# The first chunk's scores and feed-forward products from unsplit float32 operands, and a transpose in PE's transpose mode, in a bucketed attention and feed-forward kernel

## Chip, core and metric

One core of a Trainium2 chip runs the whole kernel. The metric is device time in microseconds (us) of one execution. The engines are named as in the profile: PE does matrix products (PEld are its weight loads), DVE, ACT and POOL are the vector, scalar and general engines, SP issues DMAs.

## What is computed

Attention over 4 batches, 8 heads, 768 positions and a head width of 64, in which a query sees only keys of its own hash bucket, and behind it a feed-forward block of 3072 tokens, width 512, inner width 2048:

```python
q_bits = (np.einsum('bhsd,dk->bhsk', q, proj) > 0)      # 6 bits a position, k likewise
mask = q_bucket[:, :, :, None] == k_bucket[:, :, None, :]
scores = np.where(mask, scale * np.matmul(q, k.transpose(0, 1, 3, 2)), -1000000000.0)
attn = np.exp(scores - max) / (sum + 1e-09)
x = np.matmul(attn, v)          # as [3072 tokens, 8 heads x 64]
h = x @ w_in
out = (0.5 * h * (1.0 + erf(h / sqrt(2)))) @ w_out
```

Inputs are float32, the two weights arrive as float64. The result is close to float32, so most products are made from 16-bit halves.

## The kernel before

**Passes and units.** The work goes in passes (`passes`): the first 256 queries of batch 0, the other 512 of batch 0, and then batches 1 to 3 whole. A pass goes through the eight heads, and a head through units of 128 queries by 768 keys (`unit`): 16 units in the first pass, 32 in the second, 48 in each other one, 192 in all. Queries are grouped in chunks of 256; the feed-forward part works on one chunk after the other, twelve of them.

**A head** (`head`) loads q and k of the head, transposed, as one tile of 128 partitions (`raw`, in the first pass `rawe`), takes the largest absolute value (L545), sums it over partitions on PE (L502), makes a power-of-two scale in four small DVE steps (L505 to L520), a 16-bit high half (L550) and low halves (L569 to L585), and copies halves to the other partitions by DVE, ACT, POOL or DMA (L552). The halves are projected on the hash vectors (L610), ACT takes signs (L616), and four small steps write them as extra rows beside q and k, so that a score product also adds the mask. The operands are the four tiles Aq, Ak, Bq and Bk. The first pass uses eight sets of them, of which six stay for the second pass; the two other heads are prepared again there. The sets beyond lie in the memory of x, or in a pool that is released (`go_late`) before the tiles `h` and `g` of the feed-forward part are made.

**A unit** makes scores by four 16-bit products (L824, L825), the row maximum (L828), two small steps (L832, L837), exponentials with their sum on ACT (L840), and the reciprocal of the sum (L850). Then there are two ways. The "whole" way (`whole_turn`, for all four pairs of heads in the first pass and three in the second) stays in float32: it scales the identity by the reciprocals (tile `dr`), multiplies the exponentials by it on PE, six products of 128 by 128 (L897), which transposes and divides at once, and ACT or DVE copies the result to `pt`. The other way makes high and low halves on two engines (L853, L856) and transposes them by DMA. `values` multiplies by v: twelve float32 products (L945) or 36 16-bit ones (L954) for a pair of heads and a chunk, given out in three steps, and writes x as two halves (L974, L981).

**Weights** (`weight_pair`) are decoded from float64 to float32 on DVE in place (L667 to L677), squared sums on PE give a scale (L690), and each of eight blocks of each weight is scaled into a buffer `o`, rounded and subtracted into two 16-bit halves that overwrite the float32 values.

**Feed-forward.** A chunk goes in two groups of eight inner blocks. A hidden step is twelve 16-bit products 256 wide (L1128), ACT evacuates two steps at a time (L1138) and applies Gelu to the group in the one buffer `h` (L1162), the result is split into halves `g` (L1172, L1176), and an output step is six products 512 wide (L1200). Output sums keep two of the four PSUM banks `hp` from the first group to the drain (L1221); scores of projections, transposes, values and hidden steps share the others. Before the first output product all of w_out must be split, and before a hidden product its block of w_in.

**Order.** No engine's order is written by hand. `Plan` lists steps with an engine or several that may do it, a cost, a key and the steps they need, runs through them in a model of the engines, and writes the instructions in the order found; free steps of lowest key go first. Keys are the unit's number with an offset from the table `PAR`; feed-forward steps on PE have keys from 1000 (`LATE`) on, so they come only where no attention product is ready. Each engine runs its instructions in the written order.

## Time and profile before

| | us |
|---|---|
| median of three runs | 924.03 |
| lowest and highest | 920.8, 924.16 |
| the profiled execution | 922.43 |
| its span, first to last instruction | 920.3 |

| engine | busy us | share of the span |
|---|---|---|
| PE | 852.7 | 93% |
| PEld | 577.0 | 63% |
| DVE | 732.2 | 80% |
| ACT | 615.6 | 67% |
| POOL | 376.1 | 41% |

The mean clock granted to PE is 0.983 of full speed. In the profile a line of slices gives the busy share of 40 equal parts of the span in tenths. A row of a stage has the stage's ends, its length, then busy time and number of instructions of PE, PEld, DVE, ACT and POOL, the granted clock, the share of DMA and GB/s. A row of the timeline has start, duration, engine, line, operation, output and input tile, form and count, and in brackets idle time before it and what ended it. A row of groups has line, engine, operation, tiles, form and count, then busy time and mean ns, then idle time before it. Durations on PE overlap; a float32 product shows as two records.

### The profile page before, as it was taken

The page shows a single profiled execution, that of the slowest core. Times are in us where ns is not written, and L with a number is a line of the kernel's source. Part 1 is how long each engine was busy: PE and PEld are TensorE (multiplying, and loading weights), DVE is VectorE, ACT ScalarE, POOL GpSimd, SP SyncE. Part 2 cuts the span into 40 slices and gives each one's busy share as a digit, 9 for nine tenths or more (in the row PEclk, how much of TensorE's full clock was granted, in tenths as well). Part 3 has the DMA queues.
Part 4 walks back from the last instruction along what each step waited for, and adds up shares of the span by engine and source line. Part 5 has one row for each costly group of instructions (what it writes and reads, how often), then busy time and mean ns, then how long its engine had stood idle before and what let it go on. Part 6 is the DMA issues. An engine that isn't in the chain of part 4 may idle for free. (4 is left out here: it accounts for less than half of the span.)

```text
span 920.3 us, 18292 instructions
## 1 busy us (share of the span) xinstructions
PE 852.7 (93%) x6857; PEld 577.0 (63%) x6857; DVE 732.2 (80%) x1717; ACT 615.6 (67%) x997; POOL 376.1 (41%) x356
## 2 busy tenths in 40 slices
PE   1678799989999999898999999999999999999998
PEld 0456567766667655575666666666657767576763
DVE  6899999999999999998889889999988892312122
ACT  4677898689777886866786778785985654232221
POOL 3583657285636654444256445565332310000000
PEclk9899899999999999999999999999999999999999
DMA  8634554437778787878776787696847753000000
GB/s 236 198 105 151 158 167 134 133 90 147 154 140 165 156 152 159 177 156 161 126 161 149 163 179 152 139 175 145 154 78 161 130 110 61 24 1 24 1 24 23
DMA packets 301208, 117.75 MB, mean 128 GB/s; under 512 B 241536, under 2 KB 289600, under 8 KB 301120
## 3 DMA queue, kind: packets, MB, share of 16 engines
q1 hardware_dynamic: 301040, 116.59, 58.2%
q8 instruction: 53, 0.87, 0.4%
q14 instruction: 35, 0.29, 0.1%
q10 hardware_dynamic: 80, 0.00, 0.0%
HBM read 44.31 MB, written 6.29 MB: 55 GB/s over the span
## 5 line engine op out<-in xcount | busy, mean ns | idle before, releaser
L1128 PE MATMUL hp<-x,Win 128*128 128x256 f16 x2304 | 269.2, 274 | 2.6 <-DVE o L1221 2.3
L1200 PE MATMUL hp<-Wout,g 128*128 128x512 f16 x1152 | 263.1, 380 | 0.0
L1128 PEld LDWEIGHTS <-Win 128*128 128x128 f16 x2304 | 224.8, 98 | 43.7 <-issue 7.0
L1200 PEld LDWEIGHTS <-g 128*128 128x128 f16 x1152 | 110.6, 98 | 126.0 <-issue 4.9
L828 DVE TENSOR_REDUCE rows<-s 128x1 f32<-128x768 f32 x192 | 179.2, 946 | 5.9 <-PE s L825 4.5
L840 ACT ACTIVATE p<-s,rows 128x768 f32<-128x768 f32 x140 | 138.1, 987 | 62.3 <-DVE rows L837 40.3
L1138 ACT ACTIVATE h<-hp,ffs 128x512 f32<-128x512 f32 x96 | 65.3, 682 | 104.0 <-PE hp L1128 99.9
L824 PE MATMUL s<-Ak,Aq 88*128 88x384 f16 x360 | 120.6, 335 | 12.5 <-ACT p L840 9.3
L825 PE MATMUL s<-Bk,Bq 128*128 128x384 f16 x360 | 120.4, 334 | 0.0
L394 DVE TENSOR_SCALAR g<-h,ffs 128x512 f16<-128x512 f32 x28 | 15.2, 543 | 92.7 <-ACT h L1162 59.6
L1176 DVE SCALAR_TENSOR_TENSOR g<-h,ffs,g 128x512 f16<-128x512 f32 x96 | 75.5, 800 | 15.4 <-ACT g L391 12.8
L954 PE MATMUL hp<-pt,vhl 128*64 128x256 f16 x1368 | 82.3, 274 | 3.0 <-DMA pt<-wraw 1.7
L954 PEld LDWEIGHTS <-vhl 128*64 128x64 f16 x1368 | 72.6, 110 | 15.9 <-issue 12.7
L856 DVE SCALAR_TENSOR_TENSOR hl<-p,rows,hl 128x768 f16<-128x768 f32 x73 | 78.6, 1078 | 2.9 <-POOL hl L394 1.5
L897 PE MATMUL hp<-dr,p 128*128 128x128 f32 x468 | 65.6, 296 | 6.7 <-POOL dr L394 4.9
L897 PEld LDWEIGHTS hp<-dr,p 128*128 128x128 f32 x468 | 61.0, 207 | 12.8 <-POOL dr L394 5.7
L840 ACT ACTIVATE wraw<-s,rows 128x768 f32<-128x768 f32 x52 | 51.3, 986 | 25.6 <-DVE rows L837 15.7
L394 POOL TENSOR_SCALAR hl<-p,rows 128x768 f16<-128x768 f32 x33 | 38.2, 1159 | 60.2 <-DMA pt<-hl 21.4
L825 PEld LDWEIGHTS <-Bq 128*128 128x128 f16 x360 | 35.9, 100 | 36.8 <-issue 18.8
L824 PEld LDWEIGHTS <-Aq 88*128 88x128 f16 x360 | 35.9, 100 | 30.8 <-issue 10.7
L394 POOL TENSOR_SCALAR raw<-raw,hs 64x768 f32<-64x768 f32 x41 | 45.1, 1100 | 23.9 <-ACT Aq L391 20.6
L394 POOL TENSOR_SCALAR g<-h,ffs 128x512 f16<-128x512 f32 x39 | 34.3, 885 | 40.7 <-ACT h L1162 30.8
(150 smaller groups left out, 1297.1 us busy)
## 6 DMA issues: line engine op xcount, KB each, us to landing
raw<-qk SPq DMA_DIRECT2D x26, 384.0 KB
vraw<-v SPq DMA_DIRECT2D x25, 384.0 KB
wraw<-w_in SPq DMA_DIRECT2D x16, 512.0 KB
wraw<-w_out SPq DMA_DIRECT2D x16, 512.0 KB
out<-o SPq DMA_DIRECT2D x11, 512.0 KB
rawe<-qk SPq DMA_DIRECT2D x8, 384.0 KB
vhl<-v SPq DMA_DIRECT2D x7, 384.0 KB
Ak<-Aq SPq DMA_DIRECT2D x24, 96.0 KB
```

What stands on the lines that cost most here:

```text
L394: on.tensor_scalar(out=out, in0=in_, scalar1=scale, scalar2=bias, op0=ALU.mult, op1=ALU.add)
L824: nc.tensor.matmul(to, aq[kk, qs], ak[kk, n], start=True, stop=False)
L825: nc.tensor.matmul(to, bq[:, qs], bk[:, n], start=False, stop=True)
L828: nc.vector.tensor_reduce(out=nm, in_=both(sp), axis=AX.XY, op=ALU.max, negate=True)
L840: nc.scalar.activation(out=buf(ex).rearrange("p (b k) -> p b k", b=2), in_=both(sp), func=AF.Exp, scale=sc, bias=nb, accum_out=ssum,)
L856: nc.vector.scalar_tensor_tensor(out=buf(hi)[:, 1], in0=buf(ex), scalar=r, in1=buf(hi)[:, 0], op0=ALU.mult, op1=ALU.subtract,)
L897: nc.tensor.matmul(buf(step[0])[:, (k - k0) * P : (k - k0 + 1) * P], buf(ex)[:, words(k)], buf(dg), start=True, stop=True,)
L954: nc.tensor.matmul(pv[j * D : (j + 1) * D], buf(vh)[:, tv, kt, j * D : (j + 1) * D], buf(holds[j][0])[:, tp * KT + kt, :nt], start=kt == 0 ...
L1128: nc.tensor.matmul(buf(pair[0])[:, j * ch[1] : (j + 1) * ch[1]], win_hl[:, f0 // WB1, tw, pr, f0 % WB1 : f0 % WB1 + P], x[:, tx, pr, : ch[1]],
L1138: nc.scalar.activation(out=bufs["h"][0][:, 2 * fp : 2 * fp + 2, :nt], in_=buf(pair[0])[:, : 2 * nt].rearrange("p (j k) -> p j k", j=2), fu ...
L1176: nc.vector.scalar_tensor_tensor(out=gt[:, 1, s2, :nt], in0=h[:, s2, :nt], scalar=sg, in1=gt[:, 0, s2, :nt], op0=ALU.mult, op1=ALU.subtract,)
L1200: nc.tensor.matmul(buf(banks[u]).rearrange("p (c f) -> p c f", c=NWB), gt[:, tg, f, u * P : (u + 1) * P], wout_hl[:, :, tw, ft], start=ft ...
```

## The change

- `PLAIN = (8, 0)`: in the first pass all eight heads are made by a new function, `head_plain`. q and k go by two loads to the same 64 partitions of two float32 tiles, in the memory of the four 16-bit ones. There is no scale and no halves: projection, signs and four masks only. The six kept heads serve the second pass in this form too; the other two are made there by `head`.
- A unit with such operands makes scores by two float32 products 384 wide.
- The whole way no longer scales the identity: DVE, ACT or POOL divides the exponentials in place (128 by 768), and PE transposes them with the float32 identity in its transpose mode. `WHOLE` gives it to four pairs in the first pass and two, not three, in the second.
- x of the first chunk is one float32 tile. Its hidden products use the decoded float32 w_in, its output products take Gelu's result from `h` and the decoded w_out, so `g` is not used. The splits of a block of w_in wait for the hidden products that read it, those of w_out for the chunk's last output product. The first output product needs w_out decoded, and the first one of the second chunk needs it split.
- `values` gives out its products in one step instead of three. The planner's model adds 0.095 where PE changes the shape of its tiles, some costs in it differ, and every value of `PAR` is another. The buffers `rawe` and `dr` go; a float32 identity, float32 hash vectors and one more offset tile, loaded by four DMAs from ACT's queue, come.

```diff
-WHOLE = (4, 3, 0, 0, 0)
+PLAIN = (8, 0)
+WHOLE = (4, 2, 0, 0, 0)
...
+ident32 = const.tile([P, P], F32, tag="ident32", name="ident32")
+nc.vector.tensor_copy(out=ident32, in_=ident)
...
+off = const.tile([P, 1], F32, tag="off", name="off")
+for n in range(4):
+    nc.scalar.dma_start(out=off[n * 32 : (n + 1) * 32], in_=offset[:32])
...
+def head_plain(b, h, i, key, clear, cl):
+    both_of = pairs[i]
+    loads = []
+    for k in range(2):
+        def load(k=k):
+            nc.sync.dma_start(out=both_of[k][:D], in_=qk[b, h][k * D : (k + 1) * D])
+        loads.append(add("SP", 0.75, load, key - PAR["HQ"], clear))
...
+    def project():
+        for half in range(2):
+            n = slice(half * HS, (half + 1) * HS)
+            for k, x in enumerate(both_of):
+                r0 = half * 64 + k * 32
+                nc.tensor.matmul(
+                    buf(pp)[r0 : r0 + 32, :HS], hash32, x[:D, n], start=True, stop=True, tile_position=(0, r0)
+                )
+    def sign():
+        nc.scalar.activation(out=buf(space), in_=buf(pp)[:, :HS], func=AF.Sign, bias=off)
...
+            def mask(half=half, k=k, x=x, box=box):
+                r0 = half * 64 + k * 32
+                by = (BIG / 2, -BIG / 2) if k else (0.5, 0.5)
+                affine(
+                    box[0].engine, x[rows, half * HS : (half + 1) * HS], buf(space)[r0 : r0 + 2 * NBIT], *by
+                )
...
 def scores():
...
+        if back is None:
+            q, k = (x[: D + 2 * NBIT] for x in pairs[i])
+            nc.tensor.matmul(to, q[:, qs], k[:, n], start=True, stop=True)
+            continue
...
 def whole_turn(ex, nr, r, place, cl, t):
-    def diagonal():
-        affine(dg.engine, buf(dg), ident, r)
+    def divide():
+        affine(dg.engine, buf(ex), buf(ex), r)
     def product(k0, k1, step):
         for k in range(k0, k1):
-            nc.tensor.matmul(
-                buf(step[0])[:, (k - k0) * P : (k - k0 + 1) * P], buf(ex)[:, words(k)], buf(dg),
-                start=True, stop=True,
-            )
+            nc.tensor.transpose(buf(step[0])[:, (k - k0) * P : (k - k0 + 1) * P], buf(ex)[:, words(k)], ident32)
...
+def plain():
+    affine(hi.engine, x_plain(xt[b, ch])[:, pr, :nt], buf(parts[0])[:, :nt])
...
 def hidden(j, c=c, pair=pair, b=b, ch=ch, bare=bare):
+    for pr in range(NPAIR) if bare else ():
+        nc.tensor.matmul(
+            buf(pair[0])[:, j * ch[1] : (j + 1) * ch[1]],
+            win_32[:, f0 // WB1, pr, f0 % WB1 : f0 % WB1 + P],
+            x_plain(xt[b, ch])[:, pr, : ch[1]], start=pr == 0, stop=pr == NPAIR - 1,
+        )
...
+ready = w_decoded["in"][c] if bare else [sa, w_ready["in", c // 2][1][c % 2]]
...
+if bare:
+    splits["in"][c // 2][c % 2].needs.append(pair[1])
...
 def output(f=f, ft=g * GF + f, us=us, banks=banks, bare=bare):
+    for u in us if bare else ():
+        nc.tensor.matmul(
+            buf(banks[u]).rearrange("p (c f) -> p c f", c=NWB),
+            bufs["h"][0][:, f, u * P : (u + 1) * P], wout_32[:, :, ft],
+            start=ft == 0, stop=ft == NFT - 1,
+        )
...
-        needs += out_w if n == 0 else []
+        needs += [d for ds in w_decoded["out"] for d in ds] if bare else out_w if n == NG else []
...
+if bare and g == NG - 1:
+    for ws in splits["out"]:
+        for step in ws:
+            step.needs.append(acc[0])
```

More of the change, by code (lines that the diff above doesn't have):

```diff
@@ L304, in tile_bucket_attention_moe @@
     }
[L305 to L306 removed]
+    pairs = [
+        [const.tile([P, S], F32, tag=f"{nm}{i}", name=f"{nm}{i}") for nm in ("Q", "K")] for i in range(NSET)
+    ]
     rows = const.tile([P, NT, 6], F32, tag="rows", name="rows")
@@ L938, in values, with product @@
             x_parts[b, ch] = []
-        def product(kts):
+        def product():
             pv = buf(parts[0])[:, :nt]
-            for kt in kts if whole else ():
+            for kt in range(KT) if whole else ():
                 for j in range(2):
@@ L950, in product @@
                     )
-            for kt in () if whole else kts:
+            for kt in () if whole else range(KT):
                 for ti, (tp, tv) in enumerate(TERMS):
@@ L984, in low @@
             )
-        needs = [parts[-1]] + (early_steps if (b, ch) != (0, FIRST[0][0]) else [])
+        if (b, ch) == PLAIN_CH:
+            assert whole
+            hi = add(
+                {"ACT": (0.3, PAR["XP_ACT"]), "DVE": (0.34, PAR["XP_DVE"])}, 0, plain, -10, parts[-1:]
+            )
+            free(parts[0], [hi])
+            x_parts[b, ch].append(hi)
+            for hold in holds:
+                free(hold[0], parts[-1:])
+            return parts[-1]
+        needs = [parts[-1]] + early_steps
         if whole:
```

166 lines of the change are left out of this document (101 added, 65 removed).

## The prediction

> **What bounds it now.** I read the page's slices first (busy tenths, clock granted to PE), then two stages.
>
> ```profile
> PE   1678799989999999898999999999999999999998
> DVE  6899999999999999998889889999988892312122
> PEclk9899899999999999999999999999999999999999
> ```
>
> ```profile
> 220.00:760.00 540.00, 525.10 (x4360) 348.58 (x4358) 493.34 (x1156) 402.06 (x620) 252.45 (x237) 0.99 0.76 151
> 760.00:920.30 160.30, 156.47 (x1096) 103.55 (x1094) 38.37 (x63) 43.52 (x51) 0.00 (x0) 1.00 0.08 22
> ```
>
> From 220 us on, PE (first busy column) is full but for 14.9 and 3.8 us. DVE (third) falls to 38 us after 760, where only feed-forward work is left: DVE finishes attention 160 us early, so PE sets the end. The time is PE's work plus PE's idle time, and the first slices hold most of the idle time. Why, shows PE's timeline:
>
> ```profile
> 22.90 0.50 PE L824 MATMUL s<-Ak,Aq 88*128 88x384 f16 x1
> ...
> 144.10 1.47 PE L1128 MATMUL hp<-x,Win 128*128 128x256 f16 x12 [0.28 <-DVE pt L394]
> ...
> 224.47 1.46 PE L1200 MATMUL hp<-Wout,g 128*128 128x512 f16 x6
> ```
>
> The first score comes at 22.9, the first hidden product at 144.1, the first output product at 224.5. Feed-forward work fills PE's gaps, and before 144 there is none, though x of the first chunk is complete at 115 (DVE's timeline):
>
> ```profile
> 114.54 0.47 DVE L981 SCALAR_TENSOR_TENSOR x<-hp,s_v,x 128x256 f16<-128x256 f32 x1
> ```
>
> How fast PE issues is read from start to next start, since durations overlap:
>
> ```profile
> 85.98 1.08 PE L690 MATMUL hp<-Win 128*128 128x128 bf16 x16
> 86.99 2.81 PE L945 MATMUL hp<-pt,vhl 128*64 128x256 f32 x24
> 89.73 0.34 PE L824 MATMUL s<-Ak,Aq 88*128 88x384 f16 x1
> ...
> 90.40 1.50 PE L897 MATMUL hp<-dr,p 128*128 128x128 f32 x12
> 91.78 0.32 PE L824 MATMUL s<-Ak,Aq 88*128 88x384 f16 x1
> ```
>
> ```profile
> 456.55 2.16 PE L954 MATMUL hp<-pt,vhl 128*64 128x256 f16 x36
> 458.64 1.48 PE L1128 MATMUL hp<-x,Win 128*128 128x256 f16 x12
> ```
>
> ```profile
> 814.82 5.34 PE L1200 MATMUL hp<-Wout,g 128*128 128x512 f16 x24
> 820.00 8.02 PE L1128 MATMUL hp<-x,Win 128*128 128x256 f16 x72
> 827.86 5.34 PE L1200 MATMUL hp<-Wout,g 128*128 128x512 f16 x24
> ```
>
> A unit's four 16-bit scores take 0.67 us (89.73 to 90.40), 12 fp32 records of the transposes of the attention weights 1.38 (two records a product: 0.23 a product), a whole value step 2.74, a split one 2.09, a hidden step of 12 products 1.31 (7.86/6), an output step of 6 products 1.30 (5.18/4), a bf16 product 128 wide 0.063 (1.01/16). Counts to 140 us, then from 140 to 220:
>
> ```profile
> L897 PE MATMUL hp<-dr,p 128*128 128x128 f32 x289 | 42.7, 305 | 6.1 <-POOL dr L394 4.9 <-ACT dr L391 0.9 <-ACT pt L391 0.2
> L825 PE MATMUL s<-Bk,Bq 128*128 128x384 f16 x48 | 18.2, 379 | 0.0
> L945 PE MATMUL hp<-pt,vhl 128*64 128x256 f32 x144 | 18.2, 386 | 0.8 <-DVE pt L394 0.8
> ```
>
> ```profile
> L897 PE MATMUL hp<-dr,p 128*128 128x128 f32 x180 | 23.3, 280 | 0.6 <-DVE pt L394 0.6
> L1128 PE MATMUL hp<-x,Win 128*128 128x256 f16 x158 | 19.0, 273 | 0.3 <-DVE pt L394 0.3
> L945 PE MATMUL hp<-pt,vhl 128*64 128x256 f32 x96 | 13.6, 413 | 2.7 <-DVE tiny L372 2.7
> ```
>
> At these rates the work to 140 us is 289 x 0.115 + 144 x 0.114 + 28 units x 0.67 (48 such products here, 8 from other tiles; two a unit) + about 13 of small groups = 81: 59 us idle or at a lower clock. From 140 to 220 it is 192 x 0.115 (12 records read another tile), 158 x 0.109, 96 x 0.114, 20 units, 5 of small groups = 69: 11 idle. Together **70 us**, of PE's idle time the part that the change can reach.
>
> **PE's work.** *Scores*: 40 of 192 units (16 of the first pass, 24 of the second with the six kept heads) go from four 16-bit products to two fp32 products 384 wide. By the fp32 transposes one costs 3 x 0.23 = 0.69, by four 16-bit passes 0.67. I take 1.37 a unit: +0.70 x 40 = **+28** (+27 to +29). *Feed-forward*: 16 hidden and 16 output steps of the first chunk become four products 256 wide and two 512 wide: 1.83 by a whole value step (2.74 x 4/6), 1.73 by four 16-bit passes; I take 1.80: 16 x 0.49 + 16 x 0.50 = **+16** (+14 to +18). *Transposes*: 240 products at 0.23 are 55 us; 192 remain (one pair less), in a mode that no row shows. The floor is the bf16 product, 0.063; one fp32 record is 0.115; I take 0.09: 17, so **-38** (-44 to -33; at the full 0.23 only -11). The Trainium skill (TensorE: Matmul & The Clock Gate, Terms) says that transpose mode is four times faster for fp32; an estimate by that page is 0.058 each, and the sum would be 6 us lower. No trace here shows it yet. *Values*: the moved pair saves 2 x 0.65 = **-1**. Projections get dearer by about what the eight heads' column sums save. Sum **+5**, from -4 to +13.
>
> **What leaves the other engines.** Rows to 144 us:
>
> ```profile
> L545 DVE TENSOR_REDUCE tops<-rawe 128x1 bf16<-128x768 f32 x8 | 7.6, 947 | 4.5 <-DMA rawe<-qk 4.5
> L511 DVE TENSOR_SCALAR hs<-hs 128x2 f32<-128x2 f32 x10 | 4.9, 487 | 0.2
> L576 DVE SCALAR_TENSOR_TENSOR Bk<-rawe,hs,Aq 64x768 f16<-64x768 f32 x3 | 3.6, 1185 | 0.1
> L576 DVE SCALAR_TENSOR_TENSOR Bq<-rawe,hs,Aq 64x768 f16<-64x768 f32 x2 | 2.7, 1342 | 0.1
> L394 POOL TENSOR_SCALAR rawe<-rawe,hs 64x768 f32<-64x768 f32 x11 | 12.2, 1113 | 16.5 <-DVE Aq L394 11.9 <-issue 2.0 <-ACT x L391 1.9
> L391 ACT ACTIVATE dr<-ident,rows 128x128 f32<-128x128 bf16 x13 | 5.1, 397 | 3.8 <-DVE rows L850 3.6
> L394 POOL TENSOR_SCALAR dr<-ident,rows 128x128 f32<-128x128 bf16 x11 | 4.6, 423 | 14.2 <-DVE rows L850 12.8 <-PE hp L610 1.0
> L394 POOL TENSOR_SCALAR hl<-p,rows 128x768 f16<-128x768 f32 x33 | 38.2, 1159 | 60.2 <-DMA pt<-hl 21.4
> ```
>
> DVE, at 9 in nearly every slice, loses for eight heads 7.6 + 8 x 0.49 + 6.3, four low halves of x (1.9) and smaller steps: about 24 us before x is complete. POOL loses 12 us and its subtractions. Dividing whole rows costs POOL 1.16 for 0.42 on 32 units; taking turns with ACT, whose diagonal took 0.40, it adds under 0.8 each, about 13 us in what POOL and ACT gain; without that cover it would delay each unit by 0.8. The moved pair's eight units get two halves and a DMA transpose for a division and two copies, about even; the first chunk's splits of h go. SP issues two loads a head for one and loses the copies by DMA; the four offset loads go before ACT's first work, long ahead of its first sign. First work comes earlier too:
>
> ```profile
> 5.86 0.95 DVE L545 TENSOR_REDUCE tops<-rawe 128x1 bf16<-128x768 f32 x1 [2.59 <-DMA rawe<-qk]
> ```
>
> A head has landed by 5.9 us; where a maximum, column sums, halves and copies stood before the projection, only projection, sign and four masks are left, so scores can start near 10 us. All in all x is complete near **90 us** instead of 115, and hidden products, which now need only the decoded w_in, start then instead of at 144.
>
> **PE's idle time after.** To 90 us PE has 16 units of 1.37 + 0.54 + 0.69 and about 10 us of small groups: 51, so 39 idle. To 220 it has 58 us of first-chunk feed-forward and the second pass: 24 x 1.37 + 8 x 0.67 + 16 x 0.54 + 4 x 2.74 + 4 x 2.09 and 10 small = 76; 134 us for 130, nearly full; I allow 6. A **new wait** follows: w_out is split only after the first chunk's last output product, since the split overwrites what that reads.
>
> ```profile
> L414 POOL TENSOR_TENSOR Wout<-o,Wout x8: 2123/2132/2708, 139.1 to 202.6; 128x1024 f16<-128x1024 f32 x8
> L391 ACT ACTIVATE o<-Wout,tiny x6: 1132/1138/1149, 136.4 to 200.2; 128x1024 f32<-128x1024 f32 x6
> L391 ACT ACTIVATE Wout<-o x4: 1041/1044/1047, 137.9 to 197.3; 128x1024 f16<-128x1024 f32 x4
> ```
>
> Eight splits of 1.14 + 1.04 + 2.13 = 35 us, spread over POOL, ACT and DVE, take at least 12; as each chains its three steps through two buffers I expect 30. Behind a waiting split stand the exponentials on ACT and the divisions on POOL. Meanwhile PE has a unit each 3.75 us (144 units in 540 us) with about 1.3 of work, and the eight hidden steps of the next chunk that the one h buffer allows, 10.5 us: of 30 us, 9 idle. Sum 39 + 6 + 9 = 54 for 70: **-16**. Of four hp banks, two now hold output sums during the second pass's transposes. A half takes a bank for about 1.3 us, 42 us in all, value and hidden steps another 46: 44 us on each remaining bank in some 100, so nothing; a full bank would show as PE waiting for copies.
>
> **Sum**: 922.4 (the profiled run; within 0.2% of the median 924.0) + 5 - 16 = 911. All planner keys change too, so the order after 220 may move its idle time by a few us either way.
>
> **Rivals.** *More gain*: transposes at 0.063 (-5), the w_out wait hidden (-9): 897. For: attention's lead grows; against: one h buffer. *Output waits for w_out's decoding*, which DVE did at 95 to 180 us before: hidden products fill PE from 90 to 120, then PE goes without output products for up to 30 us at a third idle: +10, 921. *The w_out split as slow as before*: the rows above span 136 to 205, 68 us. PE then has 68/3.75 x 1.3 + 10.5 = 34 of work, 34 idle for 9: 936, slower. It undoes the gain from some 48 us on. For it: one row per split on POOL, 2.1 us; against: it was spread before because nothing hurried it. *Transposes at the full fp32 price* (the mode does nothing): 192 x 0.14 = 27, half of it in the first pass's idle time: +14, 925, no change. *Clock*: slices at 8 already show the clock drop where PE is sparse. If transposes did not keep it up, 0.85 over the 125 full us from 90 would cost 19: 930, slower. By the same page of the Trainium skill (Part 4), transpose mode does not count as PE activity for the clock gate. The fp32 products between the transposes speak against that here; no row of before can show it.
>
> **Chances.** Forecast 911: 0.54; more gain 0.12; w_out decoding 0.12; slow split 0.12; full price 0.06; clock 0.04. Under 0.5% (4.6 us) a measurement of this kernel can't be told from no change. Faster 0.66, same 0.18, slower 0.16. The range, 894 to 931, takes in PE's bounds (902 to 919) and all rivals but the slow split.
>
> **What would show it.** First score near 10 us; first hidden product near 90 and first output product near 125; transposes at one record, start to start near 0.09; two fp32 scores 1.37 a unit; a dip of PE behind the first chunk's feed-forward while w_out is split; the tail after attention still full. I am wrong if x of the first chunk is no earlier than 105 us, if the dip is over 20 us, or if fp32 products cost over 0.25 for 128 columns.

## The result, and the profile after

| | before | after |
|---|---|---|
| median of six runs each, us | 923.13 | 927.9 |
| lowest and highest | 920.05, 924.82 | 924.57, 928.55 |
| profiled execution and its span | 922.43, 920.3 | 927.58, 925.8 |
| PE, DVE, POOL busy | 852.7, 732.2, 376.1 | 876.7, 729.6, 297.9 |

The changed kernel takes 1.0051 times as long as the one before (95% interval 1.0026 to 1.0075). The forecast was 911, so it is 17 us late. The time lies inside the range, but it is slower instead of faster, by about as little as the prediction said could be told at all (0.5%).

The slices of the page after the change (busy tenths of PE and DVE, clock granted to PE):

```profile
PE   7999999997967999989999999999999999999998
DVE  3798998898989999899998999998989993312122
PEclk9997999999978999999999999999999999999999
```

PE now fills at once, and the old gap ahead of slice 6 is gone. A new one stands in slices 10 to 13 (208 to 301 us), with a lower clock in the last two. The clock also falls in slice 4 (69 to 93 us). The stretches that were shown of before:

```profile
220.00:760.00 540.00, 512.79 (x4182) 337.13 (x4181) 499.05 (x1156) 408.56 (x621) 210.24 (x186) 0.98 0.73 146
760.00:925.80 165.80, 161.95 (x1162) 108.47 (x1159) 45.10 (x81) 44.16 (x53) 1.81 (x2) 1.00 0.12 29
```

PE is idle for 27.2 of the 540 us from 220 on, where it was 14.9. Its timeline at the places that the prediction named, and the last write of the first chunk's x on ACT:

```profile
60.60 1.46 PE L891 MATMUL s<-rest,x 76*128 76x384 f32 x4
61.89 0.28 PE L967 MATMUL hp<-ident,p 128*128 128x128 f32 x1
...
96.56 1.89 PE L1213 MATMUL hp<-x,Win 128*128 128x256 f32 x8
...
167.41 1.98 PE L1296 MATMUL hp<-Wout,h 128*128 128x512 f32 x4
...
300.30 1.01 PE L1303 MATMUL hp<-Wout,g 128*128 128x512 f16 x2
```

```profile
91.71 0.38 ACT L403 ACTIVATE x<-hp 128x256 f32<-128x256 f32 x1
```

x of the first chunk is complete at 92 us, the first hidden product comes at 96.6, the first output product at 167.4, and the first 16-bit output product, the second chunk's, at 300.3.

**Attention as a clock.** The best view of where the lead went is not PE's idle time but the start of attention's units. A unit's scores are four records on PE in either form, 768 for 192 units; sorted by start, every fourth begins a unit. Three kernels, in us (the third is an experiment below):

| | before | after | after, scores on 128 rows |
|---|---|---|---|
| unit 17 (second pass) | 99.6 | 80.2 | 71.5 |
| unit 49 (second batch) | 223.8 | 212.1 | 202.9 |
| unit 97 | 396.7 | 407.9 | 399.9 |
| unit 145 | 581.5 | 590.7 | 582.7 |
| end of the last value product | 774.5 | 782.6 | 773.0 |
| end of PE's work | 916.5 | 921.9 | 912.4 |

After the change attention leads by 19.4 us at unit 17 and by 11.7 at unit 49, is 11.2 behind at unit 97, and PE's work ends 5.4 later. So 7.7 us of the lead go in units 17 to 48 and 22.9, most of the loss, in units 49 to 96; 5.8 come back behind them. The same in feed-forward steps (hidden and output steps begun by a time, counted by their records):

| by | 220 us | 300 us | 400 us |
|---|---|---|---|
| before | 13 | 52 | 93 |
| after | 25 | 44 | 88 |

Twelve steps of lead turn into eight of arrears within 80 us, and into five by 400. The stretches between those units, first before and then after (columns as in the prediction: ends, length, busy time of PE, PEld, DVE, ACT, POOL, clock):

```profile
0.00:99.60 99.60, 59.33 (x449) 41.16 (x450) 85.97 (x215) 64.43 (x124) 48.77 (x57) 0.93 0.61 181
99.60:223.80 124.20, 115.61 (x992) 87.09 (x992) 118.27 (x293) 109.36 (x211) 78.05 (x67) 0.96 0.47 125
223.80:396.70 172.90, 164.71 (x1351) 104.88 (x1350) 164.04 (x390) 132.54 (x206) 89.14 (x81) 0.99 0.80 159
396.70:774.50 377.80, 371.09 (x3129) 251.84 (x3128) 329.14 (x767) 274.47 (x419) 160.11 (x153) 1.00 0.73 144
```

```profile
0.00:80.20 80.20, 70.96 (x313) 38.67 (x314) 54.91 (x149) 46.30 (x96) 15.52 (x33) 0.94 0.70 192
80.20:212.10 131.90, 126.73 (x819) 84.50 (x818) 122.74 (x294) 105.53 (x202) 66.19 (x51) 0.99 0.62 150
212.10:407.90 195.80, 169.01 (x1291) 105.22 (x1289) 179.66 (x412) 147.43 (x220) 102.95 (x82) 0.93 0.72 146
407.90:782.60 374.70, 370.68 (x3135) 251.49 (x3134) 338.31 (x793) 278.72 (x424) 113.20 (x108) 1.00 0.72 143
```

Read three things here. From unit 97 on PE is busy for 98% before and 99% after, so most of a delay at unit 97 goes to the end (in an experiment below, 22.9 of 24.5 us). In units 49 to 96 PE is not busy for 26.8 us instead of 8.2, with only 4.3 more work. And DVE does 177.7 us of work ahead of unit 49 instead of 204.2, but 518.0 from there to the last value product instead of 493.2: nearly as much as left it early comes to it later, though in other steps.

### The profile page after: what moved, and what is told of

It reads as the page before. It is cut to its first block, busy times and chain, and to the rows that moved or that the text cites. A ratio compares the mean times of both kernels' runs of the same rounds, so it can differ in the third digit from the quotient of the medians.

```text
span 925.8 us, 17374 instructions
## 1 busy us (share of the span) xinstructions
PE 876.7 (95%) x6481; PEld 570.7 (62%) x6481; DVE 729.6 (79%) x1700; ACT 610.6 (66%) x977; POOL 297.9 (32%) x274
## 5 line engine op out<-in xcount | busy, mean ns | idle before, releaser
L1222 PE MATMUL hp<-x,Win 128*128 128x256 f16 x2112 | 244.8, 273 | 3.7 <-DVE o L1333 1.3
L1303 PE MATMUL hp<-Wout,g 128*128 128x512 f16 x1056 | 243.2, 383 | 0.0
L1222 PEld LDWEIGHTS <-Win 128*128 128x128 f16 x2112 | 206.0, 98 | 41.7 <-issue 8.9
L893 PE MATMUL s<-Q 88*128 88x384 f16 x304 | 100.3, 330 | 14.0 <-ACT p L910 10.5
L894 PE MATMUL s<-K 128*128 128x384 f16 x304 | 100.1, 329 | 0.0
L426 POOL TENSOR_TENSOR K<-raw,Q 64x768 f16<-64x768 f32 x31 | 56.3, 1816 | 2.6
L891 PE MATMUL s<-K,Q 76*128 76x384 f32 x112 | 53.4, 612 | 3.9 <-ACT p L910 3.8
L894 PEld LDWEIGHTS <-K 128*128 128x128 f16 x304 | 30.0, 99 | 38.3 <-issue 21.8
L406 POOL TENSOR_SCALAR Q<-sign 24x384 f16<-24x384 f16 (+1 forms) x45 | 28.9, 642 | 67.7 <-ACT sign L628 37.5
L1259 ACT ACTIVATE h<-h 128x2048 f32<-128x2048 f32 x24 | 45.9, 1911 | 0.4
```

What stands on the lines that cost most here:

```text
L406: on.tensor_scalar(out=out, in0=in_, scalar1=scale, scalar2=bias, op0=ALU.mult, op1=ALU.add)
L426: on.tensor_tensor(out=out, in0=in0, in1=in1, op=ALU.subtract)
L893: nc.tensor.matmul(to, aq[kk, qs], ak[kk, n], start=True, stop=False)
L894: nc.tensor.matmul(to, bq[:, qs], bk[:, n], start=False, stop=True)
L1222: nc.tensor.matmul(buf(pair[0])[:, j * ch[1] : (j + 1) * ch[1]], win_hl[:, f0 // WB1, tw, pr, f0 % WB1 : f0 % WB1 + P], x[:, tx, pr, : ch[1]],
L1303: nc.tensor.matmul(buf(banks[u]).rearrange("p (c f) -> p c f", c=NWB), gt[:, tg, f, u * P : (u + 1) * P], wout_hl[:, :, tw, ft], start=ft ...
```

## The experiments

The first theory was the clock of the first pass; its rival the hand-over of w_out, PE's hole between 258 and 300 us. When neither held all of the loss, two more came: the written order by itself, and the load that the splits put on POOL, ACT and DVE. Each diff is against the changed kernel, unless it says before. Times are set beside the kernel before in the same session by the ratio; the changed kernel's own ratio is 1.0051.

### The clock in the first pass

In the changed kernel PE is busy without a gap from 19.3 to 47 us, and yet slow (its timeline):

```profile
22.02 1.49 PE L967 MATMUL hp<-ident,p 128*128 128x128 f32 x6
23.30 2.77 PE L891 MATMUL s<-K,Q 76*128 76x384 f32 x4
25.87 1.54 PE L967 MATMUL hp<-ident,p 128*128 128x128 f32 x6
...
46.65 0.87 PE L967 MATMUL hp<-ident,p 128*128 128x128 f32 x6
47.36 1.46 PE L891 MATMUL s<-K,Q 76*128 76x384 f32 x4
48.66 0.82 PE L967 MATMUL hp<-ident,p 128*128 128x128 f32 x6
```

A unit's scores take 2.57 us from 23.30 to 25.87, and 1.30 from 47.36 to 48.66: PE ran at half clock until a value step ended at 46.7. The clock column prints 1.00 for this stretch, since no change of the clock was recorded before it; only the durations show it.

**Streams on PE alone** (c1_clock). All of the kernel's work is left out.

```diff
+half_scores(90); gap(); plain_scores(24); gap(); turns(160); gap(); products(70)
+gap(); full_scores(24); gap(); unit(10)
...
```

> Attention and feed-forward are left out; PE runs streams of one kind each, with 10 us of idle time between: 16-bit products 128 by 384, float32 products of 76 rows by 384 (the plain scores), transposes in transpose mode, ordinary float32 products 128 by 128, float32 products of 128 rows by 384, units of two plain scores and six transposes; then plain scores, transposes and units behind 60 warm 16-bit products. Theory A (the clock): plain scores and transposes do not bring the clock up, so their records keep twice the length (about 0.97 us and 0.22 us apart in pairs) through a whole stream from rest, while 16-bit and ordinary float32 products of 128 rows double their speed within about 8 us. Theory B (the clock of the first 47 us was only a late start): every stream doubles its speed within 8 us.

The copies that should have made the gaps ran ahead, so PE never rested more than 0.3 us and the question of a start from rest was missed. What it gave is prices at full clock: a plain score product on 76 rows 0.652 us (24 in 15.65), on 128 rows 0.656, an ordinary float32 product 128 wide 0.227 (70 in 15.9), a transpose in transpose mode 0.110 (160 in 17.7), a unit of two scores and six transposes 1.95, steadily through ten units.

**A burst of 16-bit products at the start** (c2_warm), and **the burst with two 16-bit products ahead of each half of a unit's transposes** in the first pass (c3_warm_fill); **ordinary products by the identity in place of transpose mode** (c4_product):

```diff
+for _ in range(40):
+    nc.tensor.matmul(bufs["s"][0][:, :P], ones, ones, start=True, stop=True)
...
+            if t < 16:
+                nc.tensor.matmul(buf(step[0])[:, :P], ones, ones, start=True, stop=True)
+                nc.tensor.matmul(buf(step[0])[:, P : 2 * P], ones, ones, start=True, stop=True)
...
-nc.tensor.transpose(buf(step[0])[:, ...], buf(ex)[:, words(k)], ident32)
+nc.tensor.matmul(buf(step[0])[:, ...], buf(ex)[:, words(k)], ident32, start=True, stop=True)
```

> The changed kernel with 40 bf16 products 128 by 128 on PE before its first work, where it sits idle until 5 us; all else in the same order. Theory A (the half clock from 9 to 47 us holds up the first pass, and all later work with it): if the clock then stays up, x of the first chunk is complete 10 to 15 us earlier and the time falls by 8 to 18 us; if it drops again at once, nothing changes. Theory B (the time went into the wait for the split of w_out at 260 to 300 us): the first pass may end earlier, but the hole grows by as much, and the time stays within 3 us.

> As the run before, and two bf16 products 128 by 128 ahead of each half of a transpose in the first pass, on the bank that the transpose then overwrites. Theory A: the clock stays up from 6 us on; time 8 to 18 us under the changed kernel, less 3 us for the fillers (32 halves of 0.11 us). Theory B: within 4 us of the changed kernel.

> The changed kernel with an ordinary float32 product by the same identity in place of the transpose mode, in the same order. Theory A with transposes as what the clock gate does not count: full speed long before 47 us, and the first pass no later although each product costs 0.23 instead of 0.11; the second pass pays 96 x 0.12 = 12 us of PE, time +5 to +12 us. If plain scores are what it does not count, the clock stays down as before and the time rises by 15 to 25 us. Theory B: time +10 to +23 us, the clock as before.

The burst alone was no help: 934.63, ratio 1.0117 (1.0089 to 1.0145), with the clock at 0.5 from 10 to 40 us; why it is slower than the changed kernel no run shows. With the fillers the clock was up from 30 us on, unit 17 came at 72.8 instead of 80.2, and the profiled execution ended 6.3 us earlier; over ten runs the median was 926.54 (918.68 to 930.12), ratio 1.0035 (1.0008 to 1.0063). With ordinary products it was up at 23 us and unit 17 came at 73.8, but units 17 to 48 took 141.9 us for 131.9, since every transposing product there is dearer: 933.61, ratio 1.011 (1.0083 to 1.0138). It looked as if transposes don't raise the clock.

**The same streams from rest** (e5_rest): each waits for a chain of ACT copies that starts when the one before has ended.

```diff
+def gap():
+    nc.scalar.activation(out=chain[:, :384], in_=ps[0][:, :384], func=AF.Copy)
...
+    for _ in range(11):
+        nc.scalar.activation(out=chain, in_=chain, func=AF.Copy)
...
+    nc.scalar.activation(out=raw[:, :1], in_=chain[:, :1], func=AF.Copy)
```

> Only PE streams, each behind a rest of PE of at least 12 us that is a chain of ACT copies: 48 records of 76-row plain scores, 120 transposes, 8 units of 2 plain scores and 6 transposes, 128-row plain products 384 wide, ordinary fp32 products 128 wide, 16-bit products 384 wide, 6 units with ordinary products for the transposes. All of attention and feed-forward is left out. If transposes (and products on 76 rows) don't raise the clock, the streams of transposes and of units stay at 0.21 a transpose and 2.6 a score pair to their ends (120 transposes 25 us, 8 units 31 us), while ordinary products and 16-bit ones reach 0.227 and 0.163 within 7 us. If every stream raises the clock alike, each is at full speed within 7 us: 120 transposes in about 16 us, 8 units in about 20 us, and the slow first 47 us of the changed kernel come from something else.

PE's timeline, one row for a stream and three rows out of the units:

```profile
3.71 31.09 PE L79 MATMUL ps<-raw 76*128 76x384 f32 x48 [3.71 <-DMA raw<-qk]
47.46 14.77 PE L83 MATMUL ps<-ident,raw 128*128 128x128 f32 x120 [12.66 <-ACT raw L71]
...
98.42 2.76 PE L79 MATMUL ps<-raw 76*128 76x384 f32 x4
100.98 1.48 PE L83 MATMUL ps<-ident,raw 128*128 128x128 f32 x6
102.26 2.76 PE L79 MATMUL ps<-raw 76*128 76x384 f32 x4
...
119.19 14.62 PE L91 MATMUL ps<-raw 128*128 128x384 f32 x40 [12.88 <-ACT raw L71]
146.47 15.08 PE L87 MATMUL ps<-ident,raw 128*128 128x128 f32 x120 [12.66 <-ACT raw L71]
```

24 scores on 76 rows take 31.09 us, 1.295 each: half clock to the end of a stream without a gap. 120 transposes take 14.77, 0.123 each with the start (0.19 each for the first 3 us, 0.109 from there): they do raise it. The units stay at half clock for 31 us (3.84 from 98.42 to 102.26, where the first stream study had 1.95). The same scores on 128 rows take 0.73 each with the start. In the last stream ordinary products stand in for a unit's transposes, and there the clock is up from the second unit on (scores in 1.29 us, 208.07 to 209.36). So both theories fall in their first form: not the transposes, but the scores' 76 rows fail to raise the clock, though they keep it up once it is. Beside them the transposes, a third of a unit's time, don't raise it either; ordinary products do.

**Scores on all 128 rows** (e9_rows128): rows 76 to 127 of Q and K are set to zero, which changes nothing in the sums.

```diff
+for pair in pairs:
+    for x in pair:
+        nc.gpsimd.memset(x[D:], 0.0)
...
-q, k = (x[: D + 2 * NBIT] for x in pairs[i])
+q, k = pairs[i]
```

> The changed kernel in its own order, with the plain score products on all 128 rows (rows 76 to 127 of Q and K set to zero by 16 memsets on POOL at the start). If products on 76 rows are what keeps PE at half clock from 5 to 47 us, the clock is up by 25 us, x of the first chunk is complete 6 to 9 us earlier and the end moves by as much: 919 to 922, at least 5 us below the changed kernel's 927.9. If the rows have nothing to do with it, 927 to 930, with the half clock to 47 us as before.

918.22 us, ratio 0.9954 (0.993 to 0.9979): 9 us less than the changed kernel, and 0.5% less than the one before. PE's timeline:

```profile
14.96 2.93 PE L894 MATMUL s<-K,Q 128*128 128x384 f32 x4
...
18.85 1.56 PE L894 MATMUL s<-K,Q 128*128 128x384 f32 x4
...
23.30 0.87 PE L970 MATMUL hp<-ident,p 128*128 128x128 f32 x6 [0.63 <-DVE p L409]
24.02 1.46 PE L894 MATMUL s<-K,Q 128*128 128x384 f32 x4
```

The clock is up behind the very first scores, at 18.4 us, although these come 5.5 us later than at 9.4, for the memsets stood ahead of POOL's setup. Unit 17 is 8.7 us earlier, and 9.5 arrive at the end of PE's work.

Not all of the 8.7 is the half clock up to 47 us. In the changed kernel's profiled execution the clock falls a second time, for the scores of units 15 and 16, and in other executions of the same scores it doesn't. Unit 16, in the changed kernel and in a run below that changes nothing ahead of it (e10_split_short):

```profile
73.86 2.93 PE L891 MATMUL s<-K,Q 76*128 76x384 f32 x4 [1.23 <-ACT p L910]
```

```profile
71.49 1.56 PE L895 MATMUL s<-K,Q 76*128 76x384 f32 x4 [1.33 <-ACT p L914]
```

The profiles of c2, e11, e14 and e15 show this second fall too and have unit 17 at 78.6 to 80.0; those of e8, e10, e12 and e16 don't and have it at 76.2 to 77.1. None of the three with 128 rows (e9, e13, e18) has it. So up to 4 us at unit 17 can differ between profiled executions with the same work ahead of it.

**The memsets out of the way** (e13_rows128_early): six on DVE, ten behind POOL's setup.

```diff
+for pair in pairs[:3]:
+    for x in pair:
+        nc.vector.memset(x[D:], 0.0)
...
 on.memset(hash16, 0.0)
+for pair in pairs[3:]:
+    for x in pair:
+        on.memset(x[D:], 0.0)
```

> As with the plain scores on 128 rows, but the memsets stand where DVE and POOL are idle (six on DVE behind the projection's operands, ten on POOL behind the setup), so that the first score comes near 9.4 us again and not at 15. If the first pass is bound by PE until x of the first chunk is complete, the 5.5 us count: 911 to 916. If DVE sets the pace of the first pass once the clock is up, 916 to 919.

919.86, ratio 0.9968 (0.995 to 0.9986). The first scores come at 9.8, yet unit 17 at 71.2, only 0.3 us earlier. The clock was up for the third unit, but fell again (0.50 from 25 to 30 us, the scores at 28.7 in 2.93 us), so this run doesn't tell whether PE's first products still set the pace of the first pass once the clock is up. The two versions can't be told apart.

### Does PE's work count?

**Transpose mode alone, in the kernel before** (e6_before_turn). It leaves out the division by the row sums, for which a constant in the copy stands:

```diff
-nc.tensor.matmul(buf(step[0])[:, ...], buf(ex)[:, words(k)], buf(dg), start=True, stop=True)
+nc.tensor.transpose(buf(step[0])[:, ...], buf(ex)[:, words(k)], ident32)
...
```

> The kernel before, in its own order, with the transposes of the attention weights in transpose mode; the weights are left undivided (a constant in the copy stands for the row sums), ACT and POOL still build the diagonal. If the price of a transpose is what the step says (0.11 for 0.23) and PE sets the end, PE's work falls by 240 x 0.12 = 29 us, of which that part counts that doesn't lie in the idle time of the first 140 us (150 of the 240 stand there): 10 to 20 us less, 904 to 914. If transposes let the clock fall in the sparse first pass, the first 100 us lose as much as the later ones gain: 918 to 928. If the order around them sets the time, no change: 921 to 926.

922.63, ratio 0.998 (0.9951 to 1.0008). 240 cheaper transposes bring nothing that can be measured. Units 1 to 16 take 76.9 us (76.7 before), units 17 to 48 129.5 (124.2), while PE is less busy and its clock lower (0.83 from 50 to 140 us, before 0.91 and 0.93); how much of the gain the lower clock takes back was not tested:

```profile
50.00:90.00 40.00, 30.02 (x214) 19.11 (x213) 37.24 (x90) 31.24 (x68) 24.16 (x24) 0.83 0.47 139
90.00:140.00 50.00, 37.47 (x260) 22.48 (x260) 47.57 (x121) 43.22 (x85) 27.05 (x22) 0.83 0.53 156
```

**Plain scores as 16-bit products** (e7_scores_short):

```diff
-nc.tensor.matmul(to, q[:, qs], k[:, n], start=True, stop=True)
+q, k = (x[: D + 2 * NBIT].bitcast(BF16).rearrange("p (n t) -> p n t", t=2)[:, :, 1] for x in pairs[i])
+for m in range(2):
+    nc.tensor.matmul(to, q[:, qs], k[:, n], start=m == 0, stop=m == 1)
```

> The changed kernel in its own order, with each plain score product replaced by two 16-bit ones of the same width on the upper halves of the same operands; that leaves out the lower halves of the scores. PE's work falls by 40 units x 0.62 = 25 us. If PE's work and the clock bound the first 140 us, x of the first chunk is complete some 10 us earlier and the time falls by 10 to 20 us (908 to 918). If the order and the other engines set the time behind 90 us, only 0 to 5 us (923 to 928).

920.63, ratio 0.9972 (0.995 to 0.9993). Unit 17 is 7.9 us earlier, the end of PE's work 8.9. Units 17 to 48 keep their 131.5 us (131.9), although 24 of the 40 cheaper units stand there: of 25 us of work only those count that lay in the first pass, where PE was slow.

**Plain hidden products as one 16-bit product each** (e12_hidden_short):

```diff
-win_32[:, f0 // WB1, pr, f0 % WB1 : f0 % WB1 + P],
-x_plain(xt[b, ch])[:, pr, : ch[1]], start=pr == 0, stop=pr == NPAIR - 1,
+wa = win_32[:, f0 // WB1, pr, f0 % WB1 : f0 % WB1 + P].bitcast(BF16)
+xa = x_plain(xt[b, ch])[:, pr, : ch[1]].bitcast(BF16)
...
+wa.rearrange("p (n t) -> p n t", t=2)[:, :, 1],
+xa.rearrange("p (n t) -> p n t", t=2)[:, :, 1],
...
```

> The changed kernel in its own order, with the 64 plain hidden products of the first chunk as one 16-bit product each on the upper halves; this leaves out the lower halves. PE's work between 96 and 212 us falls by 64 x 0.34 = 22 us. If PE's work there sets the end, the time falls by 12 to 20 us (908 to 916). If DVE and the order set the pace from 90 to 220 us, PE only idles more: 0 to 5 us (923 to 928).

931.02, ratio 1.0072 (1.0041 to 1.0103): no gain from 22 us less. From 90 to 220 us PE is simply less busy and its clock lower, while DVE's times stay (the changed kernel had PE 49.59 and 71.65, DVE 47.76 and 73.21):

```profile
90.00:140.00 50.00, 40.34 (x313) 26.87 (x311) 47.44 (x114) 39.52 (x80) 22.39 (x17) 0.99 0.60 170
140.00:220.00 80.00, 63.93 (x375) 34.94 (x368) 73.96 (x172) 62.69 (x111) 44.06 (x36) 0.86 0.59 128
```

**Half of the row maximum** of the 32 undivided plain units (e15_max_short), to take work from DVE instead:

```diff
+of = both(sp)[:, :1] if back is None and whole else both(sp)
-nc.vector.tensor_reduce(out=nm, in_=both(sp), axis=AX.XY, op=ALU.max, negate=True)
+nc.vector.tensor_reduce(out=nm, in_=of, axis=AX.XY, op=ALU.max, negate=True)
```

> The changed kernel in its own order, with the row maximum of the 32 undivided plain units over one half of the scores alone (this leaves out the other half in the shift): DVE's work before 220 us falls by 32 x 0.45 = 14 us, PE's stays. If DVE sets the pace from 50 to 220 us, the time falls by 6 to 14 us: 914 to 922. If PE or the fixed order sets it, 0 to 3 us: 925 to 928.

927.06, ratio 1.0028 (1.0003 to 1.0052): about 2 us less, which the two intervals don't tell from nothing. Units 17 to 48 take 132.0 us (131.9 without the edit), though DVE's work ahead of unit 49 is 11.6 us less. Neither PE's nor DVE's busy time alone sets this stretch. What is left is the units' chain through the engines in the written order; no run shows it by itself.

### The hand-over of w_out

In the changed kernel the splits of w_out stand between 259.9 and 300 us (all rows are of one tile; first and last start):

```profile
L426 POOL TENSOR_TENSOR Wout<-o,Wout x7: 2117/2423/2857, 264.0 to 297.8; 128x1024 f16<-128x1024 f32 x7
L406 POOL TENSOR_SCALAR o<-Wout,tiny x5: 1118/1119/1706, 259.9 to 291.6; 128x1024 f32<-128x1024 f32 x5
L403 ACT ACTIVATE Wout<-o x5: 1039/1045/1057, 262.9 to 293.4; 128x1024 f16<-128x1024 f32 x5
```

**The subtraction left out** (e10_split_short) or **done twice** (e11_split_long):

```diff
+if name == "out":
...
+    on.memset(dst[:, 1], 0.0)
+    return
 subtract(box[2].engine, dst[:, 1], ...)
...
+for _ in range(1 + (name == "out")):
     subtract(box[2].engine, dst[:, 1], ...)
```

> The changed kernel in its own order, with the low halves of w_out set to zero in place of the subtraction of 2.1 to 2.9 us; this leaves out w_out's low halves. If the hand-over of w_out sets PE's hole between 257 and 300 us (theory hand-over), the first 16-bit output product comes 8 to 14 us earlier than at 300.3 and the time falls by 5 to 12 us: 916 to 923. If PE waits there for attention's own chain and the hand-over is hidden beside it (theory order), the time stays within 2 us of 928.

> The changed kernel in its own order, with the eight subtractions for the low halves of w_out done twice. Theory hand-over: the first 16-bit output product comes 15 to 25 us later, the time rises by 12 to 25 us: 940 to 953. Theory order: POOL has room, the time rises by 0 to 5 us.

Shortened: 921.63, ratio 1.0003 (0.9978 to 1.0027), but the first 16-bit output product comes only 3.6 us earlier (296.7), and of 6.5 us in the traces 3.9 lie ahead of unit 17, most of them the second fall of the clock, which the edit doesn't touch; units 49 to 96 take 189.9 for 195.8, and units 17 to 48 135.7 for 131.9. Doubled: 938.65, ratio 1.0172 (1.0147 to 1.0196), with that product at 312.4 and units 49 to 96 in 205.2. Half of each theory: the splits weigh, but less than the hand-over theory said.

**The splits earlier** (e14_no_handover): the first chunk's output products read zeros, so the splits needn't wait for them, and the order is made a second time, with the starts of the first plan as keys and earlier ones for the splits of w_out and what needs them.

```diff
-bufs["h"][0][:, f, u * P : (u + 1) * P], wout_32[:, :, ft],
+bufs["h"][0][:, f, u * P : (u + 1) * P], zero.to_broadcast([P, NWB, WB2]),
...
 steps = plan.order()
+for s, t0 in zip(splits_out, SPLIT_AT):
+    s.needs = [n for n in s.needs if n is not outs[15]]
...
+steps = plan.again(early)
```

> The changed kernel with the first chunk's output products reading a tile of zeros in place of w_out (this leaves out the first chunk's output), so that w_out's halves are made between 200 and 255 us of the order instead of behind the last of those products; only the keys of these steps and of the first products that need them are moved, the others keep theirs. Theory hand-over: the first 16-bit output product comes 12 to 18 us earlier than at 300.3, the feed-forward steps done by 300 us rise from 44 to 50 or more (before: 52), and the time falls by 7 to 15 us: 913 to 921. If the loss between 220 and 300 us comes from attention's order and DVE instead, 925 to 931, with the idle time moved elsewhere.

926.9, ratio 1.0032 (1.0009 to 1.0055). The splits run from 222 to 280 us, not by 255 as meant, and the product does come 17 us earlier:

```profile
283.17 2.75 PE L1320 MATMUL hp<-Wout,g 128*128 128x512 f16 x12
```

The steps begun by 300 us rise from 44 to 49. By 400 us they are 88 again. PE's stretches, where the changed kernel has 27.09, 40.00 and 55.19:

```profile
260.00:300.00 40.00, 29.36 (x234) 18.75 (x234) 35.27 (x76) 33.61 (x50) 18.98 (x12) 0.83 0.70 148
300.00:340.00 40.00, 37.78 (x336) 25.44 (x334) 36.51 (x88) 31.20 (x49) 16.95 (x17) 0.96 0.77 142
340.00:400.00 60.00, 51.83 (x393) 31.88 (x392) 55.14 (x131) 38.90 (x62) 25.98 (x26) 0.94 0.86 169
```

A part of the idle time has moved behind 300 us. The wait for w_out stood beside another limit, attention itself: units 49 to 96 take 197.9, and PE is not busy for 28.9 us of them.

**No split** (e16_split_off): one memset for each of the eight.

```diff
 def scaled(f=f, box=box, dst=dst):
+    if name == "out":
+        (nc.gpsimd if box[0].engine == "Pool" else nc.vector).memset(dst, 0.0)
+        return
...
```

> The changed kernel in its own order, with each of the eight splits of w_out as one memset (POOL five, DVE three) in place of its three steps; this leaves out w_out's halves. Theory load: attention's units 49 to 96, which take 195.8 us instead of 172.9 before, are held by the 37 us of split work that POOL, ACT and DVE now do between them; they shrink to 180 to 186, and the time to 912 to 918. Theory wait: only PE's wait for the halves counted, and taking it away brought nothing, so 925 to 928.

921.8, ratio 0.9989 (0.9968 to 1.001). Again 4.0 us lie ahead of unit 17, most of them the second fall of the clock. The memsets end at 290 us, and still the first 16-bit output product comes only at 297.1: in the written order it stands behind attention's products, not only behind the splits. Units 49 to 96:

```profile
209.40:404.10 194.70, 169.43 (x1290) 106.40 (x1289) 174.12 (x411) 139.47 (x215) 87.39 (x74) 0.93 0.73 147
```

DVE, ACT and POOL have 5.5, 8.0 and 15.6 us less to do, and the stretch is 1.1 us shorter. Between profiled executions that change nothing in this stretch (c2, c3, c4, e7, e9, e12, e13, e15) its length goes from 193.6 to 199.3 us, so 1.1 can't be told from nothing. Theory load falls as theory wait did. Of the runs that change the splits only e10 (189.9) and e11 (205.2) lie clearly outside that spread; why the stretch is shorter in e10, which leaves out less, isn't shown.

### Order, and load on POOL

**The same instructions in another order** (e8_other_order): 135 values of `PAR` are moved.

```diff
-SU=44.43, NM_DVE=-47.53, NM_ACT=341.12, ...
+SU=-51.6, NM_DVE=-10.4, NM_ACT=634.29, ...
```

> The changed kernel with the same instructions in another order: the keys of the order are moved at random, as long as the planner's own sum stays where it was. If the order of the work is worth as much as the change is (theory order), the time differs from 928 by over 5 us to either side. If the time comes from the work and from the wait for w_out alone (theory hand-over), it stays within 925 to 931.

929.06, ratio 1.0063 (1.004 to 1.0086). Units 17 to 48 take 133.3 us and units 49 to 96 195.9: the loss isn't an accident of one order. It is one other order only.

**POOL work put into the kernel before** (e17_before_pool):

```diff
 def exps():
+    for _ in range(8 if 49 <= t < 59 else 0):
+        nc.gpsimd.tensor_tensor(out=spare, in0=ident, in1=ident, op=ALU.subtract)
```

> The kernel before, with 80 small tensor operations on POOL (about 0.3 us each, 24 us in all) put ahead of the exponentials of its units 50 to 59, where POOL was busy half the time. Theory load: POOL's work in that stretch holds attention, units 49 to 96 take 8 to 15 us longer and the time rises by as much: 931 to 938. If POOL has room there, 923 to 926.

946.79, ratio 1.026 (1.022 to 1.0301). The operations took more than was assumed:

```profile
L843 POOL TENSOR_TENSOR spare<-ident 128x128 bf16<-128x128 bf16 x80 | 39.8, 497 | 6.0
```

Units 49 to 96 take 197.4 us for 172.9, and of these 24.5 us 22.9 arrive at the end of PE's work, although POOL is busy for only 126 of the 197 us. POOL's average share says nothing of its room: what stands ahead of a unit's division (the high halves `hl`) in its queue holds the unit. From 228 to 300 us DVE waits three times for such a high half, 14.0 us in all.

**A part of the split on DVE, with scores on 128 rows** (e18_rows128_dve):

```diff
...
+if name == "out" and n_split[0] % 2:
+    to_dve.append(lo)
...
 steps = plan.order()
+for s in to_dve:
+    s.engine = "DVE"
```

> The changed kernel in its own order with the plain scores on 128 rows, and every second subtraction of w_out's low halves on DVE (1.2 us) for POOL (2.1 us and more). Theory load: POOL loses some 8 us between 250 and 290 us and DVE, which idled 9.6 of the 80 us from 220 to 300, gains 5: units 49 to 96 are 2 to 5 us shorter, 913 to 917. If DVE's queue loses as much as POOL's wins, 917 to 921.

920.59, ratio 0.9987 (0.9962 to 1.0012), no better than without it. Units 49 to 96, first with 128 rows alone, then with the subtractions moved:

```profile
202.90:399.90 197.00, 168.26 (x1290) 105.56 (x1289) 179.50 (x407) 145.55 (x220) 104.87 (x82) 0.93 0.73 146
```

```profile
202.30:401.90 199.60, 168.83 (x1291) 105.38 (x1290) 183.02 (x410) 145.33 (x220) 95.35 (x79) 0.93 0.71 144
```

DVE has 3.5 us more, POOL 9.5 less, and the stretch is 2.6 longer, though with 128 rows alone it took 197.0 in one profile and 195.5 in the other (e13). POOL's relief brings nothing here; that DVE's load counts is suggested, not shown.

## Why the prediction was wrong, step by step

**Start of the work: right.** First score at 9.4 (forecast 10), x of the first chunk at 92 (90), first hidden product at 96.6 (90). DVE has 26.6 us less to do ahead of unit 49; the forecast had about 24, before x is complete.

**PE's work, +5: about +8.** Scores 1.29 a unit (60.60 to 61.89) for 1.37, so +25 and not +28; feed-forward 1.82 a hidden step (96.56 to 98.38) as forecast, +16; a transpose 0.118 (0.71 for six, 59.89 to 60.60) for 0.09, so 192 x 0.118 = 23 and -32 instead of -38. The Trainium skill (TensorE: Matmul & The Clock Gate, Terms) gives transpose mode a factor of four for float32; the streams show 0.110 against 0.227, a factor of two. The rival with transposes at the full price is out.

**The clock: a rival put at 0.04, wrong in its cause and its place.** It cost 8 to 9 us, by the two runs with 128 rows (e9, e13), and ahead of unit 17, where the rival had 19 us from 90 us on. That its 930 is the nearest to the measured time is luck. The Trainium skill (the same page, Part 4) says that transpose mode does not count as PE activity for the gate. Here 120 transposes from rest raised the clock; products on 76 rows did not, in 31 us, where Part 1 of that page of the Trainium skill lets one busy window of about 3.4 us do. The prediction argued that the float32 products between the transposes would keep the clock up. It was those that failed to raise it. It did not look at how the first pass begins: from rest, with 76-row products in most of PE's time.

**Output from 125 on: wrong.** The first output product came at 167.4, as in the rival of w_out's decoding, whose last step began at 162.3 (on DVE). It cost little by itself: PE was full from 90 to 140 and idle for 1.9 us from there to 167.4, where the rival had it a third idle.

**PE's idle time, -16: the step that failed.** It had two parts. The 25 us saved ahead of 220 were real at first: by then twelve more feed-forward steps had begun, and attention led by 11.7 us at unit 49. But the step counted PE's idle time as if all of it could be saved, because "PE sets the end". That holds from unit 97 on (with a tail of 142 us behind attention, not the 160 that the prediction read). Ahead of it the pace is attention's, and PE's work beside it is nearly free: 22 us less of it (hidden products) or 29 us less (transposes before) brought nothing that can be measured. The first chunk's feed-forward work, which had filled PE's gaps from 144 to about 274 us, was done by 258; the second chunk's hidden products began at 235.5 (its x was complete at 229), and its first output product came at 300. So the gap was moved from the front to 260, not closed. The third term, the 9 us of idle time in the wait for w_out's split, was mis-sized and misnamed: PE was not busy for 12.9 us in the 40 of the split itself (260 to 300), but for 26.8 in units 49 to 96 instead of 8.2, and with the splits earlier or left out 28.9 and 25.3 stayed. The rival of the slow split (34 idle, 936) came nearer in size, with the same wrong cause.

**What holds units 49 to 96 is only narrowed down.** Not the wait for w_out alone (e14, e16), not the splits' work alone (e16), not one unlucky order (e8). Most of it lies in units 61 to 77: there the lead goes from 9.4 us to 7.3 of arrears, and in e16, without any split, from 12.2 to 3.4 of arrears. PE's longest wait in these units is for a DMA transpose of attention weights, ahead of a value product:

```profile
275.94 4.05 PE L1020 MATMUL hp<-pt,vhl 128*64 128x256 f16 x35 [4.83 <-DMA pt<-hl]
```

Whether these transposes and their one queue hold attention there is a rival that no run tests. What differs besides is DVE's work in units 49 to 96, 179.7 us for 164.0. The clearest part are the low halves of the next heads; on DVE in this stretch before and after:

```profile
L576 DVE SCALAR_TENSOR_TENSOR Bk<-raw,hs,Aq 64x768 f16<-64x768 f32 x3 | 4.1, 1354 | 0.1
...
L576 DVE SCALAR_TENSOR_TENSOR Bq<-raw,hs,Aq 64x768 f16<-64x768 f32 x1 | 1.3, 1283 | 0.0
```

```profile
L588 DVE SCALAR_TENSOR_TENSOR K<-raw,hs,Q 64x768 f16<-64x768 f32 x8 | 11.7, 1464 | 0.3
```

POOL makes 10 of them here where it made 11, so of DVE's four more one was POOL's, and three are halves that fall into the stretch now. The prediction counted what DVE loses early, and those steps are gone; but the new order gives DVE others that were POOL's, whose whole work fell by 78 us. Behind unit 49 DVE has 24.8 us more: 19 low halves for 8 (24.6 us for 10.4) and 12 high halves `hl` for 2 (8.0 for 1.2) make 21 of them. That 15.7 us on an engine busy for 92% (before 95%) make most of the 22.9 is argued from these sums, not shown: no run gave those steps back to POOL, and e16 took 5.5 us from DVE for 1.1. That stays open.

**Net.** In the traces the lead of 19.4 us at unit 17 loses 7.7 up to unit 48 and 22.9 up to unit 96, and regains 3.1 up to the last value product and 2.6 in the tail behind it (139.4 us for 142.0): PE's work ends 5.4 us later. Of the 17 us between 911 and 928 the clock in the first pass makes 8 to 9 (shown). Transposes and scores make 3 in the sum of PE's work, but much of that work lies where it is nearly free. The rest is what attention loses in units 17 to 96 beyond the idle time that the forecast allowed; the runs don't part it further.

## What to carry to other kernels

Where several engines run a fixed order, mark the progress of the longest chain (here the start of each unit) in both traces before adding up one engine's idle time: work off that chain costs and saves nothing, and a lead in it can be followed to the place where it is lost. Work that fills a gap is a reserve; moving it earlier moves the gap to where it used to stand. In a stretch that begins from rest, see whether PE's products raise the clock at all, by their durations and not by the clock column; zero rows that fill the array cost PE no time and bought 8 to 9 us here.

## What the runs showed of the hardware that was not expected

- From rest, float32 products on 76 rows stay at half clock for as long as they last (1.295 us each through 31 us). On 128 rows they are at full clock within the stream (0.73 on average, 0.656 at full clock). Once the clock is up, the 76-row products keep it up (0.652 each through 15.65 us).
- Transposes in transpose mode raise the clock from rest (120 in 14.77 us, 0.19 each for 3 us and 0.109 from there), but not where they take a third of the time beside 76-row products (3.84 us a unit for 31 us). Ordinary products in their place do, within the first unit.
- A float32 product costs the same on 76 and on 128 rows (0.652 and 0.656 us, 384 wide); a transpose of 128 by 128 costs 0.110, half of an ordinary float32 product (0.227).
- The tail from the last value product to the end of PE's work is 139.4 us in the changed kernel and in each of the thirteen variants in its order, whatever was changed ahead of it (other order: 134.2), and 142.0 in the kernel before and its two variants.
- 80 operations of 128 by 128 on POOL took 0.40 to 1.0 us each, 39.8 in all, and delayed a kernel by 24 us in whose stretch POOL had been busy half the time.
